# The first 256 rows of x loaded as stored and turned by TensorE, in a fused attention and state-space kernel

## The chip, the cores and the metric

The kernel runs on one core of a Trainium2 chip. The metric is the device time of one execution in microseconds (us). The core has a matrix engine (TensorE, PE in the profile, with its weight loads as PEld), VectorE (DVE), ScalarE (ACT), GpSimd (POOL) and SyncE (SP), which issues most DMA transfers. ACT issues a few transfers too. All engines run their own instruction streams and meet at semaphores.

## What is computed

The input x has 2048 rows of 1024 values in bfloat16. The reference mixes two results with a gate per row:

```
g = sigmoid((x * gate_w).sum(-1))
a = state-space layer of x: h = Lam_bar * h + B_bar x (complex, 1024 states, 2048 steps),
    y = 2 Re(C h) + x * Dskip
b = attention of x: 32 heads of width 32, q, k, v = x @ wqkv, softmax(q k / sqrt(32)) v @ wo
out = g * a + (1 - g) * b
```

The attention has 32 x 2048 x 2048 scores, each of which needs an exponential.

## The kernel before

The heads go in 8 groups of four (128 columns of q, k or v). For one group the work is cut into 8 query units of 256 rows, and each unit into 8 **bursts** of 256 keys, 512 bursts in all. A burst (`burst`, L1803) is eight matmuls of 32x128 by 256 columns on PE (L1815), which fill four banks of PSUM (the accumulators that TensorE writes), and two exponentials on ACT of 128x1024 each (L1836; L1833 where DVE computes 256 of the columns itself). PE multiplies the exponentials by v later (L1937). The projections of the next heads, the matmuls of the state-space part (L1589, L1620, L1667) and its DVE scans run between the bursts. All instructions are laid down by a Python program in a fixed order per engine. That program keeps a model of the clock (`Clock`, L66), to which each operation is added, and reads the model only in the main loop of `build` (L1993), where it decides behind which burst each piece of background work goes.

The matmuls need x with its 1024 columns on the partitions, so x is kept transposed, as `xT` (128 partitions, 8 blocks, 2048 rows). `ld_x` (L1216) fills it with transposing DMAs from the SP queue: two of 128 rows for the first 256 rows (call these r0 and r1), then seven of 256 rows (x1 to x7). `begin` (L1242) issues in this order. On the ACT queue: the weights of k for group 0 (`ld_w(0, 1)`), those of q (`ld_w(0, 0)`), five small parameter rows (`ld_prm`, L1251: Lambda_re, Lambda_im, log_dt, Dskip, gate_w, 2 KB each). On the SP queue: r0, r1, x1, the weights of v (`wv0`, L1256), x2 to x7, then transposed rows of B (L1233) and more weights. ACT also loads its table of functions with a first small exponential (L1257). GpSimd builds the identity matrix `ident` (L1260). PE runs 12 warm-up matmuls of 512 columns on zeros (L1272).

`opening` (L1310) then writes out the first 16 bursts by hand, in the order of a string:

```python
OPENING = ("K0 B0.0 Ka1 Kb1 M B0.1 Qa1 Qb1 Va0 B1.0 Ka2 Kb2 B1.1 Vb0 Ka3 B0.2 Kb3 Va1 Ka4 B0.3 Kb4 Vb1 B0.4 ...")
```

`B0.2` is the burst of query unit 0 and keys 512 to 767. `K0` projects k and q of the first 256 rows, `Ka3 Kb3` are the two halves of the projection of k from x3 (`half256`, L1299, 256 columns wide), `Qa`, `Qb`, `Va`, `Vb` the same for q and v. `M` turns the parameter rows with a matmul, and DVE works on them afterwards. PE takes its instructions in this order, so a projection whose x has not landed holds the bursts written behind it. In `K0` before, `piece` (L1284) makes the projections 128 columns wide, k and q of r0 first, then k and q of r1; ACT copies q and DVE copies k out of PSUM, and burst B0.0 follows.

A DMA waits on the semaphores of what it depends on in its issuing queue, and what is queued behind it waits with it.

## Time and profile before

| | us |
|---|---|
| median of 3 runs | 915.81 (915.23, 915.81, 918.07) |
| profiled execution | 916.06 |
| its span, first to last instruction | 914.3 |
| ACT busy in the span | 899.6 |
| PE busy | 877.4 |
| DVE busy | 808.1 |
| POOL busy | 87.2 |

The profile is of one execution. Times in it are counted from the span's start. "Busy" counts computing instructions; an issue of a DMA is shown as work of SPq or ACTq, the queue of the engine that issues. A line of the timeline gives the start, the duration, the engine, the line of the kernel, the operation, what is written and read, how many instructions were merged, and in brackets the idle time before and what ended it. In a table of windows each row gives the length of the stretch, then busy time and count for each engine, the granted clock, the mean share of time in which the 16 DMA engines had work (over 1 where packets overlap) and GB/s.

### The profile page before, as it was taken

Reading aid. Unit: us, or ns where it says so; the run is one execution under the profiler, and the core shown is the slowest. Engines: PE = TensorE matmul, PEld = TensorE weight load, DVE = VectorE, ACT = ScalarE, POOL = GpSimd, SP = SyncE. Lnnn points to the kernel's source line nnn. Section 1 sums busy time; section 2 is a strip of 40 time slices with the busy share of each in tenths; the row PEclk is TensorE's granted clock in tenths of the full one; section 3 lists DMA queues with packets and bytes.
Section 4 is the critical chain, followed back from the end, with each engine's and each line's share of the span. In section 5 each row is a group of like instructions: output and inputs, shape, how many; then the busy total and the mean of one; then the engine's idle time right before and its main releaser. Section 6 shows DMA issues by size and latency. Waiting matters only on the chain.

```text
span 914.3 us, 34069 instructions
## 1 busy us (share of the span) xinstructions
PE 877.4 (96%) x15167; PEld 514.4 (56%) x15384; DVE 808.1 (88%) x1445; ACT 899.6 (98%) x1034; POOL 87.2 (10%) x155
## 2 busy tenths in 40 slices
PE   7899999999999999999999999999999999999996
PEld 4555754557555575555655566555655656555553
DVE  2689988999899999999999999999998888899785
ACT  6999999999999999999999999999999999999997
POOL 2000000101000001101011001010000111000010
PEclk9999999999999999999999999999999999999998
DMA  9549658640465202243022231611102123423412
GB/s 197 88 96 162 106 109 162 128 101 5 85 127 126 64 18 58 73 110 81 19 74 66 77 63 31 132 57 62 40 20 55 61 77 113 140 82 118 131 66 74
DMA packets 172275, 78.97 MB, mean 86 GB/s; under 512 B 147424, under 2 KB 156640, under 8 KB 172128
## 3 DMA queue, kind: packets, MB, share of 16 engines
q1 hardware_dynamic: 169968, 76.25, 36.8%
q8 instruction: 120, 1.97, 0.9%
q10 hardware_dynamic: 2160, 0.53, 0.3%
q14 instruction: 27, 0.22, 0.1%
HBM read 26.49 MB, written 20.97 MB: 52 GB/s over the span
## 4 chain that ended last, share of the span: by engine, by line
ACT 54%; PE 37%; DVE 4%; issue 2%; DMA 1%; SPq 1%; POOL 0%; DVEq 0%
ACT f_pt L1836 40%; ACT f_pt L1833 11%; PE f_ps L1937 10%; PE f_ps L1667 9%; PE f_ps L1815 7%; PE f_ps L1589 4%; PE f_ps L1608 3%; PE f_ps L1620 2%; ACT f_cT L1836 1%; SPq L1219 1%; ACT f_Et L1836 1%; DMA f_xT<-in_A_x_dram 1%; DVE f_xi L1824 1%; DVE f_ut L1515 0%; PE f_ps L1916 0%
## 5 line engine op out<-in xcount | busy, mean ns | idle before, releaser
L1836 ACT ACTIVATE f_pt<-f_ps 128x1024 bf16<-128x1024 f32 x718 | 692.4, 1068 | 1.5 <-PE f_ps L1815 1.1
L1937 PEld LDWEIGHTS f_ps<-f_V,f_pt 128*128 128x128 bf16 x7100 | 223.6, 96 | 92.4 <-issue 58.9
L1937 PE MATMUL f_ps<-f_V,f_pt 128*128 128x33 bf16 x7100 | 255.5, 178 | 0.2 <-ACT f_pt L1836 0.2
L1815 PE MATMUL f_ps<-f_Q,f_K 32*128 32x256 bf16 x4096 | 203.4, 273 | 10.4 <-ACT f_pt L1836 3.8
L1833 ACT ACTIVATE f_pt<-f_ps 128x768 bf16<-128x768 f32 x226 | 196.0, 867 | 0.0
L1815 PEld LDWEIGHTS f_ps<-f_Q,f_K 32*128 32x128 bf16 x4096 | 60.8, 92 | 129.5 <-ACT f_pt L1836 101.5
L1620 PE MATMUL f_ps<-f_xT,f_wb 128*128 128x512 bf16 (+1 forms) x474 | 118.5, 368 | 6.6 <-DVE f_ub L1624 1.2
L1863 POOL TENSOR_SCALAR f_xp<-f_xq 128x512 int16<-128x512 f32 x91 | 62.0, 681 | 570.3 <-DVE f_xq L1862 473.1
L1824 DVE TENSOR_SCALAR f_xi<-f_ps 128x256 int32<-128x256 f32 x226 | 95.1, 421 | 21.1 <-PE f_ps L1815 18.2
L1589 PE MATMUL f_ps<-f_xT,f_wb 128*128 128x512 bf16 (+1 forms) x426 | 107.0, 369 | 4.4 <-DVE f_xi L1824 0.3
L1524 DVE TENSOR_TENSOR_SCAN f_ht<-f_pf,f_init,f_ut 128x512 bf16<-128x512 f32 x64 | 81.0, 1274 | 0.0
L1866 DVE SCALAR_TENSOR_TENSOR f_xq<-f_xq,f_xi 128x512 f32<-128x512 f32 x113 | 78.0, 690 | 2.8
L1865 DVE SCALAR_TENSOR_TENSOR f_xq<-f_xi 128x512 f32<-128x512 uint16 x113 | 77.5, 686 | 3.2 <-POOL f_xp L1863 1.7
L1862 DVE SCALAR_TENSOR_TENSOR f_xq<-f_xi,f_xq 128x512 f32<-128x512 int16 x113 | 77.5, 686 | 2.0
L1667 PE MATMUL f_ps<-f_cT,f_hp 128*128 128x512 bf16 (+1 forms) x262 | 69.4, 361 | 2.3 <-issue 0.8
L1620 PEld LDWEIGHTS f_ps<-f_xT,f_wb 128*128 128x128 bf16 x536 | 42.3, 96 | 39.8 <-issue 8.4
L1608 PE MATMUL f_ps<-f_wb,f_xT 128*128 128x128 bf16 x896 | 59.3, 219 | 0.0
L1589 PEld LDWEIGHTS f_ps<-f_xT,f_wb 128*128 128x128 bf16 x484 | 38.1, 96 | 35.7 <-issue 7.6
L1608 PEld LDWEIGHTS f_ps<-f_wb,f_xT 128*128 128x128 bf16 x896 | 50.4, 97 | 3.9 <-issue 3.8
L1624 DVE CAST f_ub<-f_ps 128x512 bf16<-128x512 f32 x64 | 44.1, 689 | 7.8 <-PE f_ps L1620 6.5
L1515 DVE TENSOR_TENSOR f_ut<-f_ht,f_tq 128x512 f32<-128x512 bf16 x64 | 43.1, 699 | 0.6
L1726 PE MATMUL f_ps<-f_cT,f_OT 128*128 128x512 bf16 x122 | 37.0, 378 | 2.2
(152 smaller groups left out, 817.1 us busy)
## 6 DMA issues: line engine op xcount, KB each, us to landing
u_scratch<-f_ub SPq DMA_DIRECT2D x64, 128.0 KB, 2.2
f_ub<-u_scratch SPq DMA_DIRECT2D x32, 256.0 KB, 2.8
ag_scratch<-f_Ag SPq DMA_DIRECT2D x32, 256.0 KB, 2.2
f_hp<-ag_scratch SPq DMA_DIRECT2D x32, 256.0 KB, 2.9
f_wb<-in_B_wqkv_dram SPq DMA_DIRECT2D x21, 256.0 KB, 3.9
out_dram<-f_xT SPq DMA_DIRECT2D x16, 256.0 KB, 2.1
f_cT<-in_B_wo_dram SPq DMA_DIRECT2D x5, 256.0 KB, 4.3
f_tq<-in_A_x_dram SPq DMA_DIRECT2D x8, 128.0 KB, 2.3
```

Of the source, the lines that this page charges most:

```text
L1524: ops.append((1.2, 0.0, lambda ri=ri: dve(lambda e: e.tensor_tensor_scan(ht[:, ri, :], rr, ut[:, ri, :], self.init[:, ri, j:j + 1], ALU.mu ...
L1589: mms.append((1, lambda e, f, l, h, a=a, w=w: e.matmul(ps[:, bank, half(h)], w[:, a, :], xT[:, a, 512 * ch:512 * (ch + 1)][:, half(h)], st ...
L1608: m = e.matmul(ps[:, bank, 128 * q:128 * (q + 1)], xT[:, a, 128 * kt:128 * (kt + 1)], w[:, a, :], start=(a == 0), stop=(a == 7))
L1620: mms.append((1, lambda e, f, l, h, a=a: e.matmul(ps[:, 7, half(h)], bT[:, (2 * n + ri) % 3, a, :], xT[:, a, 512 * ch:512 * (ch + 1)][:, h ...
L1667: mms.append((1, lambda e, f, l, h, j=j, ri=ri, hs=hs: e.matmul(ps[:, 7, half(h)], hs[:, cols], cT[ri][:, j, 512 * cb:512 * (cb + 1)][:, h ...
L1815: m = e.matmul(ps[:, 2 * sl[h // 2] + h % 2, 256 * kl:256 * (kl + 1)], K[32 * h:32 * h + 32, g % 2, 128 * kt:128 * (kt + 1)], Q[32 * h:32 ...
L1824: first = self.dve(lambda e: e.tensor_scalar(self.xi[:, b % 2, X_COLS * n:X_COLS * (n + 1)], ps[:, 2 * s + 1, 512 - X_COLS:512], X_A, X_LO ...
L1833: self.S.op("act", lambda e: e.activation(flat(self.tile[p]), flat(ps[:, 2 * s:2 * s + 2, :]), ACT.Exp, scale=SCALE), reads=[("S", s)], wr ...
L1836: f = self.act(lambda e: e.activation(self.tile[p], ps[:, 2 * s:2 * s + 2, :], ACT.Exp, scale=SCALE), [("S", s)], [("pt", p)], "exp")
L1862: self.dve(lambda e: e.scalar_tensor_tensor(xq[:], hi, 128.0 / X_K, xq[:], ALU.mult, ALU.add), i2 + ["xq"], ["xq"], "x_q")
L1866: (0.61, DEP, lambda: self.dve(lambda e: e.scalar_tensor_tensor(xq[:], xq[:], E1 / E3 * w * w, lo, ALU.add, ALU.mult), ["xq"] + i2, ["xq"] ...
L1937: m = e.matmul(ps[:, 6, o:o + 33], self.tile[p][:, h2, 256 * kl + 128 * qt:256 * kl + 128 * (qt + 1)], V[:, g % 2, 2 * i + kl, h, :], star ...
```

## The change

The first 256 rows of x are loaded as stored, by two plain DMAs of 128 rows (256 KB each) into a part of `hp` that is free at that time; call them x0a and x0b. PE turns each with 8 matmuls against `ident` (128 columns each) into two PSUM banks. DVE copies one bank of each and ACT the other into `xT`. The projections of `K0` are then 256 columns wide, k first and then q, each as two halves; all of them wait for the four copies. The issue of x1 waits until x0a has landed. The five parameter rows are issued on the SP queue, behind x0a and x0b and ahead of x1, instead of on the ACT queue. The warm-up has 6 matmuls instead of 12. `piece` goes.

```diff
+WARM = 6
     def ld_x(self, i, eng="sp"):
-        for r, n in ((0, 128), (1, 128)) if i == 0 else ((2 * i, 256),):
-            self.dma(lambda e, r=r, n=n: e.dma_start_transpose(self.xT[:, :, 128 * r:128 * r + n], self.x2[128 * r:128 * r + n, :]),
-                     [], [("xr", r + k) for k in range(n // 128)], "ld_x", eng)
+        if i == 0:
+            for r in range(2):
+                self.dma(lambda e, r=r: e.dma_start(self.x0(r), self.x2[128 * r:128 * r + 128, :]), [], [("hp", r, 2), ("hp", r, 3)], "ld_x", eng)
+            return
+        r = 2 * i
+        self.dma(lambda e: e.dma_start_transpose(self.xT[:, :, 128 * r:128 * r + 256], self.x2[128 * r:128 * r + 256, :]),
+                 [("hp", 0, 2)] if i == 1 else [], [("xr", r), ("xr", r + 1)], "ld_x", eng)
+    def x0(self, r):
+        return self.hp[:, r, 2:4, :].rearrange("p j n -> p (j n)")
+    def turn(self, r):
+        S, ps = self.S, self.ps
+        for h in range(2):
+            def mm(e, h=h):
+                m = None
+                for a in range(4):
+                    m = e.matmul(ps[:, 2 * r + h, 128 * a:128 * (a + 1)], self.x0(r)[:, 512 * h + 128 * a:512 * h + 128 * (a + 1)], self.ident[:], start=True, stop=True)
+                return m
+            S.op("pe", mm, reads=[("hp", r, 2), ("hp", r, 3), "ident"], name="turn", **(dict(acc=[("S", r)], writes=[("turn", r, 1)]) if h else dict(writes=[("S", r), ("turn", r, 0)])))
+        for h, eng in enumerate((self.dve, self.act)):
+            src = ps[:, 2 * r + h, :].rearrange("p (a n) -> p a n", a=4)
+            dst = self.xT[:, 4 * h:4 * h + 4, 128 * r:128 * (r + 1)]
+            fn = (lambda e, dst=dst, src=src: e.activation(dst, src, ACT.Copy)) if h else (lambda e, dst=dst, src=src: e.tensor_copy(dst, src))
+            eng(fn, [("S", r), ("turn", r, h)], [("xr", r) if h == 0 else ("xr1", r)], "turn")
...
-                     [], [("prm", i)], "ld_prm", "act")
+                     [], [("prm", i)], "ld_prm")
...
-            for k in range(12):
+            for k in range(WARM):
...
             if op == "K":
-                for a, b in zip(self.piece(1, 0, 7, True), self.piece(0, 0, 6, True)):
-                    a()
-                    b()
+                self.turn(0)
+                self.turn(1)
+                for part in (1, 0):
+                    for half in range(2):
+                        self.half256(part, 0, half, 6 + part)
```

`half256` takes the bank as an argument now, and for i == 0 reads `("xr1", 0)` and `("xr1", 1)` too.

More of the change, by code (lines that the diff above doesn't have):

```diff
@@ L1282, with half256 @@
                "B0.5 Kb6 Vb2 Ka7 B0.6 Kb7 Va3 B0.7 Vb3 Qa2 Qb2 B1.3 Va4 Vb4 B1.4 Qa3 Qb3 Va5 B1.5 Vb5 B1.6 Va6 Vb6 B1.7 Va7 Vb7 G")
-    def piece(self, part, i, bank, first):
-        ps, xT = self.ps, self.xT
-        w = self.w_of(0, part)[0]
-        for h in range(2):
-            r = 2 * i + h
-            def mm(e, r=r, h=h):
-                m = None
-                for a in range(8):
-                    m = e.matmul(ps[:, bank, 128 * h:128 * (h + 1)], w[:, a, :], xT[:, a, 128 * r:128 * (r + 1)], start=(a == 0), stop=(a == 7))
-                return m
-            kw = dict(writes=[("bank", bank)]) if h == 0 else dict(acc=[("bank", bank)])
-            yield lambda mm=mm, kw=kw, r=r: self.S.op("pe", mm, reads=[("w", 0, part), ("xr", r)], name="proj", **kw)
-    def half256(self, part, i, half):
+    def half256(self, part, i, half, bank=7):
         ps, xT = self.ps, self.xT
@@ L1305, in mm @@
             for a in range(4 * half, 4 * half + 4):
-                m = e.matmul(ps[:, 7, 0:256], w[:, a, :], xT[:, a, 256 * i:256 * (i + 1)], start=(a == 0), stop=(a == 7))
+                m = e.matmul(ps[:, bank, 0:256], w[:, a, :], xT[:, a, 256 * i:256 * (i + 1)], start=(a == 0), stop=(a == 7))
             return m
-        self.S.op("pe", mm, reads=[("w", 0, part), ("xr", 2 * i), ("xr", 2 * i + 1)], name="proj", **(dict(acc=[("bank", 7)]) if half else dict(writes=[("bank", 7)])))
+        self.S.op("pe", mm, reads=[("w", 0, part), ("xr", 2 * i), ("xr", 2 * i + 1)] + ([("xr1", 0), ("xr1", 1)] if i == 0 else []), name="proj", **(dict(acc=[("bank", bank)]) if half else dict(writes=[("bank", bank)])))
     def opening(self):
```

## The prediction

> **What bounds the kernel now.** I read the chain of waits for the whole span first, then ACT by windows, then the chain and the timeline of the first 20 us, where the whole change lies.

> ```profile
> ACT 54%; PE 37%; DVE 4%; issue 2%; DMA 1%; SPq 1%; POOL 0%; DVEq 0%
> ```
> ```profile
> 0.00:10.08 10.08, 1.87 (x4) 1.00 0.94 191
> 10.08:20.00 9.92, 9.69 (x13) 1.00 1.18 202
> 20.00:907.50 887.50, 886.37 (x1015) 1.00 0.37 84
> 907.50:914.33 6.83, 1.64 (x4) 0.75 0.30 111
> ```

> The second view is ACT alone, cut at its first exponential and at its last: stretch, length, busy time. From 20 us to 907.5 us ACT idles 1.1 us in all (887.50 - 886.37). The stretch is 97% of the span, and the change takes no work out of it. So the end moves by as much as ACT's stream of exponentials moves at about 20 us. Between 10.08 and 20 us ACT idles 0.23 us (9.92 - 9.69), and before 10.08 us it waits for the first projections. The change can gain in two places: a first exponential ahead of 10.08 us, and the 0.23 us. Both are needed, since a stream that starts earlier and is held at 18 us gains nothing.

> What holds it there is told by the chain of the opening, in order of time (start, duration, what):

> ```profile
> 0.91 1.37 SPq L1219
> 2.34 1.61 SPq L1219
> 3.99 2.98 SPq L1219
> 7.02 0.58 SPq L1256
> 7.65 2.82 SPq L1219
> 10.51 6.28 DMA f_xT<-in_A_x_dram
> 18.93 0.60 PE f_ps L1306 x4
> 19.91 3.77 ACT f_Et L1836 x4
> ```

> The chain does not start with the first exponential. It runs along the SP queue: the issues of r0, r1, x1, the weights of v, x2, then x3, which is issued at 10.51 and lands 6.28 us later, at 16.79. It goes on over a projection and burst B0.3 to ACT at 19.91. The timeline agrees:

> ```profile
> 17.83 1.94 ACT L1836 ACTIVATE f_OT<-f_ps 128x1024 bf16<-128x1024 f32 x2 [0.18 <-PE f_ps L1815]
> 18.90 0.34 PEld L1306 LDWEIGHTS f_ps<-f_xT,f_wb 128*128 128x128 bf16 x4 [0.29 <-DMA f_xT<-in_A_x_dram]
> ```

> ACT was idle 0.18 us before B0.2, which PE issues behind the projection from x3, and PE waited for x4 at 18.90. So two chains meet at 18 to 20 us with under 0.25 us between them: ACT's own, from 10.08 on, and SP's deliveries of x3 and x4. The end moves by the later of the two.

> **The change part by part.** First the SP queue. It loses two transposing issues, 1.37 and 1.61 us, and gets two plain issues, five small ones and a wait. The prices:

> ```profile
> L1696 SPq DMA_DIRECT2D f_tq<-in_A_x_dram x8: 328/330/574, 711.1 to 751.0; - x8
> ...
> DMA to landing us min/median/max: 2.1/2.3/3.6
> ```
> ```profile
> L1251 ACTq DMA_DIRECT2D f_ht<-in_A_Lambda_re_dram x1: 992/992/992, 1.9 to 1.9; - x1
> L1251 ACTq DMA_DIRECT2D f_ht<-in_A_Lambda_im_dram x1: 314/314/314, 2.9 to 2.9; - x1
> ```
> ```profile
> f_wb<-in_B_wqkv_dram ACTq DMA_DIRECT2D x1, 256.0 KB, 3.3
> ```
> ```profile
> f_hp<-ag_scratch SPq DMA_DIRECT2D x32, 256.0 KB, 2.9
> ```

> L1696 loads 128 rows of x as stored, half as wide: 0.33 us to issue. Two of these from 0.91, with gaps of 0.06, end at 1.63. A parameter row costs 0.31 us and 0.04 of gap, so five end at about 3.4; if the first takes 0.99, as it did on ACT, 4.1. Then x1 waits for x0a. Behind this wait in the queue stand x1, the weights of v, x2 to x7 and the rows of B, and PE waits for each x in turn. How soon does a plain 256 KB land here? From below 2.1 us (the fastest half-size load), 2.9 us (256 KB in quiet), from above 5.9 us (r0's transposing load, issued at 0.91, which PE gets at 6.77 in a row below). I take 3.3 us, the weights of k, since they have this size and are in flight in the same microseconds. So x0a lands at 4.2, the small rows are hidden behind the wait (were x0a to land before 3.4, they would set x1's issue instead), and x1 is issued at 4.25 instead of 3.99: +0.26.

> Some of that comes back. x1's issue took 2.98 us with r0, r1 and the weights still in flight:

> ```profile
> L1233 SPq DMA_TRANSPOSE f_wb<-in_A_B_re_dram x32: 1237/1250/2235, 23.6 to 585.4; - x32
> ```

> 128 rows transposed cost 1.24 us to issue when nothing presses, so 256 rows 2.48 (an estimate by doubling). With plain loads ahead of it, I put x1's issue between 2.48 and 2.98, at 2.7, and x2's between 2.48 and 2.82, at 2.65. The weights of v are then issued at 7.0, as before, and x3 at 10.51 - 0.02 - 0.17 = about 10.3. So x3 and x4 come **0.2 us earlier**. Bounds: x0a at 3.0 or before, both issues at 2.48: 3.4 instead of 3.99, and 0.50 and 0.34 saved, 1.4 us earlier. x0a at 6.77 with x1's and x2's issues at 2.48: 2.8 - 0.8 = 2.0 us later.

> One more thing shapes x3's landing (columns: PE, PEld, DVE, ACT, POOL, clock, DMA share, GB/s):

> ```profile
> 15.00:16.00 1.00, 0.93 (x16) 0.53 (x16) 0.30 (x2) 1.00 (x2) 0.00 (x0) 1.00 1.11 36
> ```
> ```profile
> q8 instruction: 1, 0.02, 10.7%
> ```

> At 15 to 16 us the DMA engines are occupied but move 36 GB/s; the mean of 10 to 20 us is 202. The only thing new, in the DMA view of 14 to 15 us, is a packet of the instruction queue. x3 lands 6.28 us after issue, where x1 took 5.1:

> ```profile
> L1219 SPq DMA_TRANSPOSE f_xT<-in_A_x_dram x1: 2985/2985/2985, 4.0 to 4.0; - x1
> ...
> DMA to landing us min/median/max: 5.1/5.1/5.1
> ```

> I leave this stall where it is: PE's stream ahead of it gets 12 instructions shorter (the warm-up loses 6 matmuls and 6 weight loads; the 32 matmuls and 32 loads of `piece` give way to 16 and 16 to turn and 16 and 16 to project), and x3 moves by tenths. If it missed x3, x3 would gain 1.2 us.

> Now the way to the first exponential:

> ```profile
> 6.77 1.05 PE L1294 MATMUL f_ps<-f_xT,f_wb 128*128 128x128 bf16 x16 [1.14 <-DMA f_xT<-in_A_x_dram]
> 8.00 1.07 PE L1294 MATMUL f_ps<-f_xT,f_wb 128*128 128x128 bf16 x16 [0.18 <-DMA f_xT<-in_A_x_dram]
> 9.10 0.38 ACT L1320 ACTIVATE f_Q<-f_ps 128x256 bf16<-128x256 f32 x1 [3.31 <-PE f_ps L1294]
> 9.96 1.05 PE L1306 MATMUL f_ps<-f_xT,f_wb 128*128 128x256 bf16 x8
> 10.08 1.94 ACT L1836 ACTIVATE f_pt<-f_ps 128x1024 bf16<-128x1024 f32 x2 [0.59 <-PE f_ps L1815]
> ```
> ```profile
> L1624 DVE CAST f_ub<-f_ps 128x512 bf16<-128x512 f32 x64 | 44.1, 689 | 7.8 <-PE f_ps L1620 6.5
> ```

> Before: the last projection ends at 9.07, the first exponential starts 1.01 us later. After: x0a at 4.2; 8 matmuls of 128 columns, most of them still at half clock as the warm-up's rows below have it (0.43 us for 512 columns, so 0.107 for 128), 0.75 us, and 0.2 for the last to come out (the eight of L1306 take 1.05 us, of which 8 x 0.107 is 0.86): 5.15; DVE's copy of 128x512 costs 0.69 us, twice over: to 6.55, if x0b and its matmuls are in by 5.85, when the second begins. ACT's copies, between 0.38 us for 256 columns and 1.0 for 1024, take 0.6 and lie beside. Sixteen projections of 256 columns take 1.05 us for the first eight and 0.87 for the next: 8.5. With the same 1.01 us, the first exponential starts at **9.5, 0.6 us earlier**. The parameter rows leave ACT's queue, so its table load comes some 2 us sooner; its next job, the copies, waits for x0a, so that is worth nothing. Six warm-up matmuls fewer are worth nothing either, since PE waits for x0a in any case.

> **The sum.** ACT's own chain: -0.6 us. SP's chain: -0.2 us, and the later one counts. The profiled execution of 916.06 us becomes 915.86; the median of the runs shown is 0.25 lower, so 915.6. Of the 0.6 us, 0.4 go into a longer idle time before B0.2.

> **The rivals.** First, **the whole gain stays**: x0a lands near 3.4, or the stall misses x3, so SP's chain is no longer the later one. Then the end moves by 0.6 us and the 0.23 us of idle time: 915.0; at its bound, with x0a at 3.0, both chains are 1.4 us earlier or more: 914.4. For it speaks that the bound from below for x3 is 1.4 us earlier; against it, that weights and x press on the DMA engines together.

> Second, **x1 is held on SP** (slower). If x0a lands no sooner than r0 did, at 6.77, x3 comes 2.0 us later and PE waits for it: 917.8. The point from which the change loses is x0a at about 4.45; each microsecond beyond costs one. For it speaks that half of the bytes needed for K0 are weights in the same engines; against it, the 0.33 us against 1.24 us of issue, and 2.9 against 5.9 to landing. [...]

> Third, **PE is still cold**. The warm-up before:

> ```profile
> 1.26 4.37 PE L1275 MATMUL f_ps<-f_hp 128*128 128x512 bf16 x12 [1.26 <-DVE f_hp L1246]
> 4.22 0.15 PEld L1275 LDWEIGHTS f_ps<-f_hp 128*128 128x128 bf16 x1 [0.28 <-issue]
> 4.60 0.53 PEld L1275 LDWEIGHTS f_ps<-f_hp 128*128 128x128 bf16 x3 [0.24 <-issue]
> ```
> ```profile
> 902.25:905.67 3.42, 1.85 (x49) 1.00 0.23 81
> 905.67:909.08 3.41, 3.00 (x38) 0.50 0.21 77
> 909.08:912.50 3.42, 1.19 (x6) 1.00 0.31 116
> ```

> The loads come 0.43 us apart up to 4.22 and closer from 4.60, so the clock rose at about 4.5. Six matmuls end near 3.85. At the end of the kernel the clock falls to 0.50 after a stretch with 1.85 us of work in 3.42 and is back after one with 3.00. Six matmuls and the turn give about 2.9 us in the stretch up to 4.55, close to the 3.00 that sufficed. Were it cold up to 8.5, 16 projections cost 1.7 us more and the second turn 0.4: the first exponential at 11.6, 1.5 late, less 0.23: 917.1. [...]

> **How the numbers follow.** Forecast 0.62, the whole gain 0.15, x1 held 0.10, PE cold 0.10; 0.03 for the modelled clock of the program, to which the new operations are added, and which could put background work of the main loop in another order. That cannot gain over the 1.1 us that ACT idles there. A measurement of this kernel can tell about 0.3%, or 2.7 us, from no change: every case taken alone lies within that, so only a sum of mishaps, or the reordering, is outside: faster 0.04, same 0.89, slower 0.07. The range goes from the bound of the first rival, 914.4, to 918.1: the second rival gives 917.8, and the kernel before reached 918.07 in one of its runs.

> **What would show it.** Right: x0a lands near 4.2; SP issues x1 right after; two DVE copies of 0.69 us; projections of 256 columns near 0.11 us each; the first exponential at 9.2 to 9.8; ACT idle 0.4 to 0.7 us before B0.2; x3 landing 16.3 to 16.9. Wrong: no idle time before B0.2 and the end 0.6 us or more earlier (first rival); x1 issued after 5 us (second); projections 0.21 us apart (third); ACT idle over 1.5 us after 20 us (the order changed).

## The result, and the profile after

The changed kernel takes 921.94 us (median of 5 runs, 921.14 to 922.78), the kernel before 916.24 us on the same chip (5 runs, 915.23 to 918.07). The ratio is 1.0061, with a 95% interval of 1.0046 to 1.0076: slower by 5.7 us, and outside the range of the prediction. The profiled execution took 921.14 us. The heads of the two pages, before and after:

```profile
span 914.3 us, 34069 instructions
```
```profile
span 919.4 us, 34061 instructions
```

The shares of the chain of waits do not show it, since 5 us are half a per cent. They stand as they stood:

```profile
ACT 54%; PE 38%; DVE 4%; issue 2%; DMA 1%; POOL 0%; SPq 0%; DVEq 0%
```

ACT by windows does show it. The cuts are again at the first and the last exponential (stretch, length, ACT busy and count, clock, DMA share, GB/s; the clock column reads 1.00 until the first change of clock is recorded, so its first row says nothing of a cold start):

```profile
0.00:13.36 13.36, 3.06 (x5) 1.00 0.86 196
13.36:20.00 6.64, 6.64 (x9) 1.00 1.40 201
20.00:909.91 889.91, 889.04 (x1020) 1.00 0.36 83
909.91:919.40 9.49, 1.63 (x4) 0.86 0.24 87
```

The first row has grown from 10.08 to 13.36 us: the first exponential is 3.28 us later, not 0.6 earlier. The second has no idle time left (6.64 of 6.64; 0.23 us before), so ACT's own chain now sets the pace and SP's deliveries are waited for no more. The third is as full as before, with 0.87 us idle instead of 1.13. The fourth has grown too, from 6.83 to 9.49 us, and that is behind the last exponential, where the prediction did not look. The last operation of the computation there is the copy of a flag by DVE, before and after:

```profile
911.08 0.14 DVE L2301 CAST flag<-f_ps 1x1 int32<-1x1 f32 x1
```
```profile
913.47 0.13 DVE L2312 CAST flag<-f_ps 1x1 int32<-1x1 f32 x1
```

It comes 2.39 us later. From its start to the end of the span were 3.2 us (914.3 - 911.08) and are 5.9 (919.4 - 913.47). So the 5.1 us of the span are two things of nearly the same size: **2.4 us that come from the opening, and 2.7 us between the last operation and the end.**

The opening first. Its chain after, in order of time:

```profile
0.91 0.40 SPq L1221
1.31 0.06 issue
1.37 5.55 DMA f_hp<-in_A_x_dram
6.92 0.05 issue
6.97 1.05 PE f_ps L1237 x8
8.02 0.02 issue
8.04 0.70 DVE f_xT L1243
8.74 0.09 issue
8.83 3.53 PE f_ps L1315 x16
```

The chain does not go along the SP queue any more. It goes over x0b, which lands at 6.92, its turn, its copy, and 16 projections that take 3.53 us, where the two rows of L1294 before took 2.12 for as much work. The timeline has the warm-up, x1's issue and the two turns:

```profile
1.25 2.74 PE L1299 MATMUL f_ps<-f_hp 128*128 128x512 bf16 x6 [1.25 <-DVE f_hp L1270]
4.87 2.12 SPq L1224 DMA_TRANSPOSE f_xT<-in_A_x_dram  x1
4.90 1.04 PE L1237 MATMUL f_ps<-f_ident,f_hp 128*128 128x128 bf16 x8 [0.91 <-DMA f_hp<-in_A_x_dram]
6.97 1.04 PE L1237 MATMUL f_ps<-f_ident,f_hp 128*128 128x128 bf16 x8 [1.03 <-DMA f_hp<-in_A_x_dram]
```

16 projections in 3.52 us are 0.22 us each for 256 columns: half clock (in e9 below the clock column reads 0.50 where such a row takes 3.42 us; in e1 the row takes 1.91), the "0.21 us apart" by which the prediction would tell its third rival. The trace records the changes of the clock: it opened at 12.17 us (at 4.55 before), and in both traces the changes lie 3.41 us or a multiple of it apart (before: 4.55, 905.67, 909.08 and 912.49 us; after: 12.17 and 916.70). Cut in steps of 3.41 us back from 12.17, PE was busy so long:

```profile
1.93:5.34 3.41, 2.50 (x10) 1.00 0.89 234
5.34:8.76 3.42, 1.63 (x14) 1.00 1.00 233
8.76:12.17 3.41, 3.34 (x16) 1.00 1.09 229
```

A stretch with 2.50 us of work did not open it, the next one even less, and the third, full of cold projections, did.

Now the end. A few records that no view counts as busy tell what each engine does there: a branch, and behind it a last `DRAIN` (starts in us):

```
          branch: SP     ACT    POOL   DVE    PE      DRAIN: SP     ACT    POOL   DVE    PE
before          913.43 913.43 913.44 913.45 913.49         913.95 913.91 913.91 914.06 913.95
after           915.81 916.11 915.83 915.84 915.87         916.34 919.11 916.30 916.44 916.34
```

Before, every engine goes on 0.5 to 0.6 us after its branch. After, four do and ACT does not: 3.00 us pass, and its branch itself is 0.3 us late. The others wait for it at the end: their last records, on semaphores, start at 919.22 to 919.35 us, behind ACT's `DRAIN` at 919.11 (before, at 914.14 to 914.28). ACT's program is the one that has changed in length: five DMA issues fewer (the parameter rows) and two copies more, so that this branch is the 1088th of its instructions in the trace instead of the 1091st. It jumps over a spare program, which did not run. Both kernels announce it by a hint (`BRANCH_PREFETCH_HINT`) 274 instructions ahead, at 686.40 us before and 688.93 after.

### The profile page after: what moved, and what is told of

It is laid out like the page before. It is cut to its first block, busy times and chain, and to the rows that moved or that the text cites. A ratio compares the mean times of both kernels' runs of the same rounds, so it can differ in the third digit from the quotient of the medians.

```text
span 919.4 us, 34061 instructions
## 1 busy us (share of the span) xinstructions
PE 878.2 (96%) x15161; PEld 515.3 (56%) x15378; DVE 809.4 (88%) x1447; ACT 900.4 (98%) x1036; POOL 87.2 (9%) x155
## 4 chain that ended last, share of the span: by engine, by line
ACT 54%; PE 38%; DVE 4%; issue 2%; DMA 1%; POOL 0%; SPq 0%; DVEq 0%
ACT f_pt L1847 40%; ACT f_pt L1844 11%; PE f_ps L1948 10%; PE f_ps L1678 8%; PE f_ps L1826 7%; PE f_ps L1600 4%; PE f_ps L1619 3%; PE f_ps L1631 3%; ACT f_cT L1847 1%; ACT f_Et L1847 1%; DVE f_xi L1835 1%; DMA f_hp<-in_A_x_dram 1%; ACT f_OT L1847 1%; PE f_ps L1927 0%; DVE f_ut L1526 0%
## 5 line engine op out<-in xcount | busy, mean ns | idle before, releaser
L1635 DVE CAST f_ub<-f_ps 128x512 bf16<-128x512 f32 x64 | 44.1, 689 | 7.9 <-PE f_ps L1631 6.5
## 6 DMA issues: line engine op xcount, KB each, us to landing
f_ub<-u_scratch SPq DMA_DIRECT2D x32, 256.0 KB, 2.8
ag_scratch<-f_Ag SPq DMA_DIRECT2D x32, 256.0 KB, 2.2
f_hp<-ag_scratch SPq DMA_DIRECT2D x32, 256.0 KB, 3.0
f_wb<-in_B_wqkv_dram SPq DMA_DIRECT2D x21, 256.0 KB, 3.7
out_dram<-f_xT SPq DMA_DIRECT2D x16, 256.0 KB, 2.1
f_cT<-in_B_wo_dram SPq DMA_DIRECT2D x5, 256.0 KB, 2.9
```

## The experiments

The theory for the time behind the flag was that it depends on where in ACT's program the last branch stands, for the opening that the half clock (six warm-up matmuls) costs what the first exponential lost. The rivals were the parameter rows' place on SP, x1 held by x0a, and x0b's late landing. Unless said otherwise the edit is made to the changed kernel. All ratios are to the kernel before, with its runs on the same chip (medians 916.2 to 916.4 us); intervals are 95%.

**e1, twelve warm-up matmuls.**

```diff
-WARM = 6
+WARM = 12
```

> The changed kernel with 12 warm-up matmuls again. Theory (six leave the clock at half speed through K0): the eight matmuls of the second turn take 0.6 instead of 1.04 us and the 16 projections 1.9 instead of 3.52, so the first exponential comes 2.1 us earlier, at about 11.3 instead of 13.36; the loss of 2.8 us behind ACT's last branch stays; time 919.5 to 920.2. Rival (the late loads and the held SP queue set the opening): first exponential at 13 or later, time 921.5 to 922.5.

919.43 us, 1.0034 (1.0023 to 1.0045): 2.5 us less than the change. The projections and the first exponential:

```profile
8.59 1.91 PE L1315 MATMUL f_ps<-f_xT,f_wb 128*128 128x256 bf16 x16 [0.98 <-DVE f_xT L1243]
11.51 1.94 ACT L1847 ACTIVATE f_pt<-f_ps 128x1024 bf16<-128x1024 f32 x2 [0.59 <-PE f_ps L1826]
```

1.91 us instead of 3.52, and the first exponential 1.85 us earlier. The loss behind the flag stays (912.14 to 918.87 us, 6.7). The clock is one cost, and there is another.

**e2, an attempt to lengthen ACT's program by empty instructions.**

```diff
             loc = []
+            if name == "act":
+                for _ in range(3):
+                    e.nop()
```

> The changed kernel with three empty instructions at the head of ACT's stream, which has 3 fewer than before. Theory (the place of ACT's last branch in its instruction stream costs 2.8 us at the end, since what follows it has to be fetched): ACT's last DRAIN comes under 0.3 us behind its branch, as before, instead of 3.0; first exponential unchanged at 13.4; time 919.0 to 919.6. Rival (the late end comes from the later opening or from chance): still 3 us, time 921.5 to 922.5.

920.87 us, 1.0051 (1.0038 to 1.0064). The trace has none of the empty instructions: ACT's first DMA issue starts at 0.80 us as in the change, its branch is again the 1088th of its instructions, and its `DRAIN` comes 3.22 us behind. They seem to have been left out of the program. If so, this is the change once more, and says nothing on the theory.

**e3, parameter rows back on the ACT queue.**

```diff
-                     [], [("prm", i)], "ld_prm")
+                     [], [("prm", i)], "ld_prm", "act")
```

> The changed kernel with the five parameter rows on the ACT queue again. Theory: x1 is held by x0a until 4.85 in any case, so the opening is as in the changed kernel, first exponential at 13.2 to 13.5; ACT's stream has 2 instructions more than before instead of 3 fewer, and if the place of the last branch matters the end costs 0 or 2.8 us. Rival (the rows on the SP queue delay what is behind them): x1 issued 1 us earlier and the first exponential 1 us earlier.

918.66 us, 1.0027 (1.0017 to 1.0037). The first exponential comes at 13.26 us, 0.1 earlier than with the rows on SP, and x1 is issued at 4.72 instead of 4.87: in the opening the rows cost nothing on SP. What went is the loss at the end (flag at 913.51, end of the span at 916.75 us: 3.2 us). The branch is ACT's 1093rd instruction here.

**e4, the kernel before with six warm-up matmuls.**

```diff
-            for k in range(12):
+            for k in range(6):
```

> The kernel before with 6 warm-up matmuls instead of 12, nothing else. Theory (six do not open the clock): the 32 projections of 128 columns take 1.7 us instead of 1.05 and 1.07 per 16, the first exponential comes 1.0 to 1.5 us later than 10.08, no loss at the end; time 917.0 to 917.8. Rival (six suffice when the loads come as before): first exponential at 10.1, time 916.0 to 916.6.

917.75 us, 1.0019 (1.0010 to 1.0028), no loss at the end.

```profile
6.75 3.57 PE L1294 MATMUL f_ps<-f_xT,f_wb 128*128 128x128 bf16 x32 [2.75 <-DMA f_xT<-in_A_x_dram]
11.33 1.94 ACT L1836 ACTIVATE f_pt<-f_ps 128x1024 bf16<-128x1024 f32 x2 [0.59 <-PE f_ps L1815]
```

So the warm-up alone, with nothing else of the change, has cold projections and a first exponential 1.25 us later, and costs 1.5 us by the medians. (The profiled execution was a quick one, 916.17 us: it had made good the delay by its last exponential. The median says that most did not; no trace shows where those lost it.)

**e5, ACT's program three instructions longer.** The small exponential that loads ACT's table is issued four times; its result is used by nothing.

```diff
         act(lambda e: e.activation(self.cm[:, 0, 0:1], warm[:, 0:1], ACT.Exp), ["warm"], [("cm", 0)], "table")
+        act(lambda e: e.activation(self.cm[:, 0, 0:1], warm[:, 0:1], ACT.Exp), ["warm"], [("cm", 0)], "table")
```

(the added line three times)

> The changed kernel with three more small exponentials (128x1, 0.2 us each) behind ACT's table load, at a time when ACT waits; ACT's stream is then as long as before the change. Theory (the place of ACT's last branch in its instruction stream decides whether what follows it has to be fetched): ACT's last DRAIN comes under 0.6 us behind the branch instead of 3.0, first exponential still at 13.3, time 918.4 to 919.4. Rival (anything else in the changed program makes the late end): DRAIN still 3 us behind, time 921 to 922.

918.39 us, 1.0022 (1.0013 to 1.0031), 3.5 us less than the change, with work added. The first exponential stays at 13.22 us. The flag and the span:

```profile
913.61 0.14 DVE L2315 CAST flag<-f_ps 1x1 int32<-1x1 f32 x1
```
```profile
span 916.9 us, 34064 instructions
```

The flag is no earlier than in the change, and the end follows 3.2 us later, as before. Three more instructions on ACT, 900 us earlier, and the loss behind the branch is gone.

**e6, the kernel before with the parameter rows on SP.**

```diff
-                     [], [("prm", i)], "ld_prm", "act")
+                     [], [("prm", i)], "ld_prm")
```

> The kernel before with the five parameter rows on the SP queue, behind r1 and ahead of x1, nothing else. Theory on the queue: x1 is issued 1.7 us later than 3.99, x3 lands 1.5 to 2 us later, the tenth exponential starts 1 to 2 us later than 19.91. ACT's stream has 5 instructions fewer than before, 2 fewer than the changed one; if every place from the changed kernel's downwards costs the fetch at the end, the last DRAIN of ACT comes 3 us behind its branch: time 918.5 to 920.5; if not, 916.5 to 918. Rival (the rows hide behind the transposes): 916.2 and no change at x3.

917.03 us, 1.0009 (1.0000 to 1.0018); no loss at the end, with the branch at place 1086 of ACT's instructions: so not every shorter program loses. The opening shows the two chains of the prediction apart:

```profile
5.79 1.91 SPq L1219 DMA_TRANSPOSE f_xT<-in_A_x_dram  x1
9.61 1.94 ACT L1836 ACTIVATE f_pt<-f_ps 128x1024 bf16<-128x1024 f32 x2 [0.59 <-PE f_ps L1815]
19.05 1.94 ACT L1836 ACTIVATE f_OT<-f_ps 128x1024 bf16<-128x1024 f32 x2 [0.98 <-PE f_ps L1815]
```

The first exponential is 0.47 us earlier than before, and the gain is lost: x1 is issued 1.80 us later, and at B0.2 ACT now waits 0.98 us where it waited 0.18. B0.2 comes 1.2 us later than before (19.05 against 17.83), as a later SP chain would have it.

**e7, the weights of q issued behind the table load on ACT.**

```diff
-        self.ld_w(0, 0, "act")
...
         act(lambda e: e.activation(self.cm[:, 0, 0:1], warm[:, 0:1], ACT.Exp), ["warm"], [("cm", 0)], "table")
+        self.ld_w(0, 0, "act")
```

(both now ahead of the parameter rows)

> The changed kernel with the weights of q issued on ACT behind its table load instead of ahead of it. Theory (x0b waits for its turn behind the weights of q, which were issued before it, and the bytes of both): x0b lands 0.7 to 1.5 us earlier than 6.9, the first exponential comes as much earlier, 12.0 to 12.7; time 920.0 to 921.3. Rival (x0b is late for itself): x0b still lands at 6.8 or later, time 921 to 922.

921.74 us, 1.0058 (1.0044 to 1.0072). The edit hardly moved what it was to move:

```profile
1.27 1.28 ACT L1273 ACT_TABLE_LOAD   x1 [1.27 <-PEq L2415]
1.34 0.53 ACTq L1252 DMA_DIRECT2D f_wb<-in_B_wqkv_dram  x1
```

ACT issues the weights 0.07 us after the start of the table load, not behind its end at 2.55. x0b's turn starts at 7.07 (6.97). Nothing follows for x0b.

**e8, x1 issued without waiting for x0a.**

```diff
-                 [("hp", 0, 2)] if i == 1 else [], [("xr", r), ("xr", r + 1)], "ld_x", eng)
+                 [], [("xr", r), ("xr", r + 1)], "ld_x", eng)
```

> The changed kernel without x1's wait for x0a; x1 writes other columns, so nothing else changes. Theory (K0 sets the first exponential, and x1 is not late for anything behind it): x1 is issued at 3.9 instead of 4.87, the first exponential stays at 13.3 or comes later by up to 0.5 since x1's packets press on x0b; time 921.3 to 922.8. Rival (the SP queue held by the wait is the loss): the end 1 us earlier, 920.9 or less.

921.41 us, 1.0053 (1.0039 to 1.0066): no gain. x1 goes 1.03 us earlier, and its issue takes 3.18 us instead of 2.12:

```profile
3.84 3.18 SPq L1224 DMA_TRANSPOSE f_xT<-in_A_x_dram  x1
7.02 1.03 PE L1237 MATMUL f_ps<-f_ident,f_hp 128*128 128x128 bf16 x8 [0.99 <-DMA f_hp<-in_A_x_dram]
```

The first exponential stays at 13.44. The wait on SP, the second rival, is not what the time went to.

**e9, the weights of q on the SP queue, behind x0b.**

```diff
-        self.ld_w(0, 0, "act")
+        self.ld_w(0, 0)
```

> The changed kernel with the weights of q issued on the SP queue behind x0b, instead of on ACT ahead of it. Theory (x0b's packets start only when the 256 KB issued before them, the weights of q, have had their turn): x0b's copy into xT can start 0.7 to 1.5 us earlier, its turn at 5.5 to 6.2 instead of 6.97, and the first exponential at 11.9 to 12.7 instead of 13.36. ACT's stream is one instruction shorter than in the changed kernel, so the end may cost 0.5 or 3 us: time 917 to 918 or 920 to 921. Rival (x0b takes this long for itself): its turn at 6.8 or later, first exponential at 13.2 or later.

918.74 us, 1.0026 (1.0016 to 1.0037), in which two things are mixed: ACT has one instruction less, its branch at place 1087, and there is no loss at the end; and x0b is earlier. The chain:

```profile
1.37 4.83 DMA f_hp<-in_A_x_dram
6.19 0.05 issue
6.24 0.64 PE f_ps L1237 x8
```

x0b lands 4.83 us after its issue instead of 5.55, so 0.7 us of its lateness came from the weights of q ahead of it. In the change, x0a's packets run from 2.96 to 4.30 us and x0b's from 4.69 to 6.38, though both were issued by 1.9, and packets of the weights on ACT's queue run beside them from 1.93 to 6.62. In e9 the latter end at 4.83, and the packets of x0a and x0b run without a break from 2.94 to 5.63. The projections are cold again (3.42 us), and the first exponential is at 12.12. The clock did an odd thing:

```profile
1.05:4.46 3.41, 2.74 (x6) 1.00 0.54 156
4.46:7.88 3.42, 1.43 (x18) 1.00 1.01 233
7.88:11.29 3.41, 3.23 (x16) 0.50 1.05 189
```

It opened at 4.46, behind 2.74 us of work, ran open while the second turn went through (0.64 us instead of 1.05), closed at 7.88 behind 1.43 us of work, just ahead of the projections, and opened again at 11.29.

**e10, both costs taken away: e1 and e5 together.**

> The changed kernel with 12 warm-up matmuls and with the three small exponentials on ACT: both costs found so far taken away. Theory (the clock costs 2.5 us and the end 3 to 3.5 us, and they add): 921.9 - 2.5 - 3.3 gives 916.1, range 915.5 to 917.0, first exponential at 11.5, last DRAIN of ACT under 0.6 us behind the branch. Rival (a third cost in the main loop, such as another order of the background work): 917.5 or more.

916.67 us, 1.0006 (0.9996 to 1.0016): no difference from the kernel before.

```profile
0.00:11.12 11.12, 3.67 (x9) 1.00 0.83 195
11.12:20.00 8.88, 8.88 (x11) 1.00 1.08 191
20.00:907.50 887.50, 886.57 (x1017) 1.00 0.37 84
907.50:914.31 6.81, 1.64 (x4) 0.89 0.31 115
```
```profile
6.75 0.64 PE f_ps L1237 x8
7.38 0.02 issue
7.41 0.70 DVE f_xT L1243
8.11 0.09 issue
8.20 1.92 PE f_ps L1318 x16
```

The two costs close the sum. The last window is 6.81 us, as before (6.83). The first exponential is at 11.12, still 1.04 us later than before, since x0b lands hardly sooner (6.70 us); but 0.43 us of this comes out of ACT's idle time in the two middle windows (0.93 us together, 1.36 before), and its 1028 operations there, as many as before, take 0.61 us less (895.45 against 896.06), which the runs do not explain. The last exponential starts at 906.36 us, 0.09 later than before.

**e11, the kernel before with three of the five parameter rows on SP**, so that ACT's program is three instructions shorter and nothing else of the change is there.

```diff
-                     [], [("prm", i)], "ld_prm", "act")
+                     [], [("prm", i)], "ld_prm", "act" if i < 2 else "sp")
```

> The kernel before with three of the five parameter rows on the SP queue: ACT's stream is 3 instructions shorter, so its last branch has the same place as in the changed kernel; nothing else of the change is in it. Theory (the place alone costs the end): ACT's last DRAIN comes 2.5 to 3.2 us behind its branch, time 918.5 to 919.8, although the opening is at most 1 us later at the tenth exponential. Rival (the late end needs something else of the change): DRAIN 0.5 us behind, time 916.2 to 917.2.

919.32 us, 1.0036 (1.0023 to 1.0049): 2.9 us slower. The opening, the flag and the span:

```profile
10.02 1.94 ACT L1836 ACTIVATE f_pt<-f_ps 128x1024 bf16<-128x1024 f32 x2 [0.59 <-PE f_ps L1815]
911.02 0.13 DVE L2301 CAST flag<-f_ps 1x1 int32<-1x1 f32 x1
```
```profile
span 917.6 us, 34286 instructions
```

Everything up to the flag is within 0.1 us of the kernel before (10.08, 911.08), and the end comes 3.3 us later. ACT's branch is at 913.67 and its `DRAIN` at 917.28. The place 1088 is enough to lose it.

**e12, twelve warm-up matmuls, the weights of q on SP, and four small exponentials more on ACT** (the branch at place 1091): the best version that the runs pointed to.

> The changed kernel with 12 warm-up matmuls, four small exponentials on ACT and the weights of q on the SP queue behind x0b; ACT's last branch has the place that it had before the change. Theory: first exponential at 10.3 to 11.0 if x0b lands earlier, no loss at the end, time 915.3 to 916.5, no worse than the kernel before. Rival (the weights of q, issued later, are late for K0): first exponential at 11.3 or later, time 916.5 to 917.5.

916.53 us, 1.0007 (0.9999 to 1.0016).

```profile
5.64 1.06 PE L1237 MATMUL f_ps<-f_ident,f_hp 128*128 128x128 bf16 x16
10.60 1.94 ACT L1851 ACTIVATE f_pt<-f_ps 128x1024 bf16<-128x1024 f32 x2 [0.59 <-PE f_ps L1830]
```

x0b is there when x0a's turn is done, and all 16 matmuls go in one row, as the prediction had wanted. The first exponential is 0.5 us earlier than in e10 and still 0.5 later than before. It is no better than the kernel before; no version was.

All 14 kernels by the place of the last branch among ACT's instructions in the trace, with the time from that branch to the `DRAIN`:

```
1086: e6 0.48
1087: e9 0.47
1088: after 3.00, e1 3.77, e2 3.22, e7 3.77, e8 3.75, e11 3.62
1091: before 0.48, e4 0.48, e5 0.48, e10 0.48, e12 0.48
1093: e3 0.48
```

The traces hold one thing more: packets of an instruction queue (q14), 8 KB each. Counted from ACT's last branch, they start so (us; "ahead" is the last 10 us):

```
1086, 1087 (2 kernels)   none ahead                   four behind, 1.08 to 1.28
1088 (6 kernels)         none ahead                   four behind, 0.67 to 1.12, a fifth 3.60 to 4.51
1091, 1093 (6 kernels)   one ahead, by 2.58 to 3.24   four behind, 1.08 to 1.51
```

The eight kernels that do not lose have four packets behind the branch. The six that lose have none ahead of it and five behind it, the first four of them while ACT stands. The change and e5 differ in three of ACT's instructions alone, and e5 has the packet ahead of the branch, so this packet goes with ACT's program. The author's guess is that ACT waits for instructions that come too late at 1088. No run shows it: the trace does not tell for which engine a packet is, the kernels at 1086 and 1087 have no packet ahead either and lose nothing, and the first four have ended 1.6 to 2.4 us before the late `DRAIN`.

## Why the prediction was wrong, point by point

**"The parameter rows leave ACT's queue ... so that is worth nothing."** This step failed, and with it the sum that knew only two chains at 18 to 20 us. On the way to the first exponential it is worth nothing, as said (e3: 13.26 against 13.36 us). But with the copies it makes ACT's program three instructions shorter, and at that place of its last branch ACT loses about 3 us behind the end of the work: 3.5 us from the change to e5, 2.8 from e1 to e10, 2.9 in the kernel before (e11). No term of the sum lay behind the last exponential. Its windows held the stretch, 6.83 us of the span, and it was taken as fixed.

**"Six warm-up matmuls fewer are worth nothing either, since PE waits for x0a in any case."** This step failed too. They do not delay x0a; they are what opened the clock. Without them it opened at 12.17 instead of 4.55 us, so that the turn of x0b took 1.04 us instead of 0.64 and the projections 3.53 instead of 1.92 (e10): 2.0 us on the way to the first exponential. By the medians, 2.5 us from the change to e1, 1.7 from e5 to e10, 1.5 in the kernel before (e4). The third rival had this mechanism and nearly its size (1.7 and 0.4 us, the first exponential at 11.6), with a chance of 0.10. It was held down by "2.9 us in the stretch up to 4.55, close to the 3.00 that sufficed", which took the stretch of the run before for that of every run, and counted a turn that came later (4.90 us instead of 4.2). In six of the seven other kernels with six matmuls, as in the change, the clock opened at 10.6 us or later. In the one where it opened at 4.46 it was closed again before the projections (e9). So cold projections came in all eight kernels with six matmuls (3.42 to 3.57 us), and were not a case of one in ten.

**x0b "in by 5.85" failed.** It landed at 6.92, and its turn ended at 8.02, 2.2 us past the mark; the half clock is 0.4 of that. The sum had a price for x0a (landed 4.86, forecast 4.2) and none for x0b, which was issued 0.46 us behind it on the same queue and landed 2.1 us later. Its 5.55 us from issue to landing are hardly less than r1's transposing load took before (5.61). 0.7 us comes from the weights of q (e9); the rest is open. Together with the clock this accounts for the first exponential: forecast 9.5, plus about 1.8 for x0b, plus 2.0, is 13.3 (13.36). In the time x0b hardly counts: e10 still has it late, and is 0.3 us above the kernel before, no clear difference.

**What was right.** x1 is held by x0a and little else: issued at 4.87 (forecast 4.25), and x1's issue gives most of the time back, so that x3 is issued at 10.66 (10.3). Two terms were off there without harm. x1's issue took 2.12 us, below the 2.48 that doubling gave as its bound. And x3 landed at 15.90, not at 16.3 to 16.9: 5.24 us after its issue, so the stall did not stay where the sum left it. SP's chain was earlier by 0.9 us at x3, not by 0.2. x1's wait is not on the path (e8). A copy of 128x512 on DVE takes 0.69 us, 16 projections with an open clock 1.92 (e10; forecast 1.05 + 0.87). No other order of the main loop cost anything, since e10 closes the sum. And a gain at the first exponential alone is lost again at B0.2 when SP's chain is later (e6). The reverse holds as well: of 3.28 us at the first exponential 2.50 reach the last one (908.77 against 906.27), and of 1.04 in e10 0.09.

**What stays open.** Why 1088 and neither 1087 nor 1091, and what ACT waits for behind that branch. That it waits for instructions is a guess from the packets of q14, and no run shows it. 1089 and 1090 were not tried, and neither was another place of the hint, which is 274 instructions ahead of the branch in all 14 kernels.

## What to carry to other kernels

Matmuls on zeros ahead of the first transfer were not idle filler here: with six of the twelve gone the projections took 3.57 us, and the kernel before lost 1.5 us (e4). Before taking any away, ask whether the work between the start and the first long row of matmuls would still open the clock, wherever the 3.41 us stretches of the trace lie. Where changes of a third of a per cent count, compare the time from the last operation to the end of the span as well: here three instructions fewer on one engine moved it by 3 us, and three cheap ones more moved it back. Here a load that was issued 0.46 us behind another landed 2.1 us behind it; give each its own price.
